# Window attention with routed experts: rows kept in 32-feature blocks, and slots turned in place by VectorE

## The chip, the cores and the metric

The kernel runs on one core of a Trainium2 chip. The metric is the device time of one execution in microseconds (us). Before the change three runs took 627.72, 629.17 and 631.42 us, a median of 629.17 us.

The engines are TensorE (PE in the profile; PEld is its weight loads), VectorE (DVE), ScalarE (ACT), GpSimd (POOL) and SyncE (SP), which issues most of the DMAs. SBUF is the memory on the core, with 128 partitions; PSUM is where PE writes its results.

## The reference

First a causal attention with a window of 64 over q, k, v of shape (8, 8, 576, 64); then each of the 4608 rows of 512 features goes through one of eight experts, chosen by a router.

```python
scores = scale * np.matmul(q, k.transpose(0, 1, 3, 2))
rel = pos[:, None] - pos[None, :]
mask = (rel >= 0) & (rel < window)
scores = np.where(mask, scores, -1000000000.0)
...
x = np.ascontiguousarray(attn_out.transpose(0, 2, 1, 3)).reshape(B * S, H * D)
logits = x @ w_gate + modality_bias[modality_id]
e_idx = np.argmax(logits, axis=1)
...
for e in range(E):
    mask = e_idx == e
    h = np.maximum(x[mask] @ w1[e], 0.0)
    out[mask] = gate_w[mask, None] * (h @ w2[e])
```

Here w1 is (8, 512, 1024) and w2 is (8, 1024, 512).

## The kernel before

**Attention steps.** Time goes in steps `s`. Step `s` forms the scores of 128 rows (`scores`, L647), their masked minima (`minima`, L661) and exponentials; one step later PE transposes the exponentials (`probs_t`, through `turn`, L481), two steps later come the values (`values`, L699) and `values_out`, which divides by the sums and writes the 128 rows as `xa` (L707, 128x512). PE transposes `xa` (`x_t`) and `logits` multiplies with the gate weights `wg` and adds the bias into `lg` (L729). Transposes, logits and routing share the PSUM banks `tp`, taken in turn, two of them; a bank that one reader still needs holds up the next writer. Tiles keep the same few names in the whole program (`tp`, `em`, `y`, `sp`), since buffers are used again.

**Routing.** `route1` to `route3` choose the expert and the place of each row. GpSimd writes the rows, `ROW` = 514 floats each (512 features, the gate value, the row's number), to `xs_scratch` in DRAM by an indirect DMA (L800). Each expert owns a region there.

**Slots.** A slot is 256 rows of one expert. `fetch` asks for the next slot and `load_slot` (L214, on SP) brings its rows into `xt`, of which there is one buffer. `slot_pieces` is a generator: from step `FIRST` = 12 on, four of its pieces are run in the gaps of each step (`gap`), between pieces of attention, and a slot takes 16 pieces. When the attention is over (about 340 us), slots run alone up to the end. There are 17 full slots and one of 128 rows.

The rows of a slot must have features on partitions for PE. A float32 product is made of three, with each operand split into a high part and a rest (`split`: ScalarE's cast L195, VectorE's subtraction L196; `xh` and `xl`). `first` multiplies with w1 (L318), ScalarE takes the positive part `hh` (L326), VectorE makes its rest `hl` (L327), and `second` multiplies with w2 (L340). The weights come in chunks of 128x512 floats (`load_piece`, L103), and are split too (L114, L119).

How `xt` is turned depends on when the slot is fetched. While `last` is not set, which holds for the first eight slots, `xt` comes in one DMA, and PE transposes it in two groups of four 128x128 pieces into PSUM (`x_turn`, L281), each with every fourth feature (`xt[:, t, c:DM:NC1]`); w1 is stored to match, in the order `(p c)`. Later slots come in four quarters of 32 partitions and one small DMA for the last two columns, and VectorE turns their 32x32 blocks into PSUM (L276). The casts of x are appended to `later`, a list which `run_later` empties at the end of a gap, behind what the gap's matmuls need.

The attention's q and k are loaded by SP too (L591 and, for the later groups, eight DMAs in quarters, L597); VectorE turns those quarters with one transpose of 128x512 (L575). Each engine works through its own instructions in the order of the program, and so does SP with its DMA issues.

```python
sl = fetch()
x_part(sl, 0)
x_part(sl, 1, ps_m.tile([P, 512], F32, name="y1"))
```

This is how the first slot starts, at step 12.

Of the kernel before, what the change touches and what calls it, by code (L numbers as in the profile page):

```python
# [8 lines left out]
F32 = mybir.dt.float32  # L9
F32R = mybir.dt.float32r  # L10
# [9 lines left out]
P = 128  # L20
# [6 lines left out]
def tile_window_attn_moe(  # L27
# [63 lines left out]
    Wlo = [wpool.tile([P, 2 * WC], F32R, name=f"Wlo{x}") for x in range(2)]  # L91


    w1_v = w1.rearrange("e (p c) f -> e p c f", p=P)
    w2_v = w2.rearrange("e (c p) f -> e p c f", p=P)

    PIECE_ORDER = (0, 2, 4, 6, 8, 9, 1, 3, 5, 7, 10, 11, 12, 13, 14, 15)
# [102 lines left out]
        assert (sl["buf"], c) not in pieces + [r[1:] for r in raws + halves]  # L200
        assert sl["any"] is None or (sl["any"], c) not in [w[2:] for w in swaps]

    def load_slot(row_ap, late, nb, quarters):
        rb = nc.values_load(row_ap, engines=[ET.SP], min_val=0, max_val=DUMMY)
        xt = epool.tile([P, 2, ROW], F32, name="xt")
        rows = xs_blk[bass.ds(rb, nb)]
        if not quarters:
            parts = [(xt[:, 0:nb], rows.rearrange("b p c -> p b c"))]
        else:
            parts = [(x_of(xt)[r * R32:(r + 1) * R32, 0:nb].rearrange("p b w d c -> p b w (d c)"),  # L210
                      rows[:, :, r * P:(r + 1) * P].rearrange("b (w p) c -> p b w c", p=R32)) for r in range(NR)]
            parts.append((tail_of(xt)[:, 0:nb], rows[:, :, DM:ROW].rearrange("b p c -> p b c")))
        for dst, src in parts:
            ins = nc.sync.dma_start(out=dst, in_=src)  # L214
            if late is not None:
                tc.declare_no_dep(ins.ins, group=late, reason="rows written before are read")
                tc.add_to_no_dep_group("early_loads", ins.ins)
        return xt

    def x_of(xt):  # L220

        flat = xt.rearrange("p b c -> p (b c)")
        return flat[:, 0:2 * DM].rearrange("p (b w d c) -> p b w d c", b=2, d=R32, c=NC1)
# [26 lines left out]
    def fetch():  # L250
        if fetched:
            return fetched.pop(0)
        row, late, buf, whichever, need = todo.pop(0)
        assert late is not None or not pads
        assert late is None or late in scattered
        tick(need - issued[0], table=True)
        nb = 1 if whichever == NANY else 2
        quarters = bool(last)
        xt = load_slot(row, late, nb, quarters)
        return dict(xt=xt, buf=buf, any=whichever, nb=nb, quarters=quarters,  # L260
                    tail=tail_of(xt) if quarters else xt[:, :, DM:])

    def slot_pieces():


        def x_turn(sl, i, tp=None):

            xt, nb = sl["xt"], sl["nb"]
            if ("tp", i) in sl or nb == 1 and i == 0:
                return  # L270
            tp = sl["tp", i] = tp or bank(2 if i and (last or not sl["quarters"]) else 0)
            cs_ = range(2 * i, 2 * i + 2) if nb == 2 else range(NC1)
            for n, c in enumerate(cs_):
                cols = slice(n * nb * P, (n + 1) * nb * P)
                if sl["quarters"]:
                    nc.vector.transpose(  # L276
                        out=tp[:, cols].rearrange("p (w t) -> p w t", t=R32),
                        in_=x_of(xt)[:, 0:nb, :, :, c].rearrange("p b w d -> p (b w) d"))
                    continue
                for t in range(nb):  # L280
                    nc.tensor.transpose(  # L281
                        out=tp[:, cols][:, t * P:(t + 1) * P].bitcast(F32R),
                        in_=xt[:, t, c:DM:NC1].bitcast(F32R), identity=ident_r)

        def x_split(sl, i):

            nb = sl["nb"]
            x_turn(sl, i)
# [4 lines left out]
            hi, lo = (x[:, (2 * i * TP if nb == 2 else 0):][:, 0:512] for x in sl["x"])  # L293
            split(sl.pop(("tp", i)), hi, lo)
            if i == 1:
                sl["gate"] = epool.tile([P, 2], F32, name="gate", bufs=2)
                nc.gpsimd.tensor_copy(out=sl["gate"][:, 0:nb], in_=sl["tail"][:, 0:nb, 0])
                sl["id"] = epool.tile([P, 2], I32, name="id", bufs=2)
                nc.gpsimd.tensor_copy(out=sl["id"][:, 0:nb], in_=sl["tail"][:, 0:nb, 1])

        def x_part(sl, i, tp=None):
            if not sl["quarters"]:
                x_turn(sl, i, tp)
            later.append(lambda: x_split(sl, i))
# [77 lines left out]
        def half_second(sl, a):  # L382
# [5 lines left out]
            for m, (w, n, c, lo) in enumerate(mm):  # L388
# [5 lines left out]
                    start=(m == 0), stop=(m == len(mm) - 1))  # L394
            id2 = epool.tile([P, 1], I32, name=f"id{a}")
            nc.gpsimd.tensor_scalar(
                out=id2, in0=sl["tail"][:, 0, 1:2], scalar1=2.0, scalar2=float(a),
                op0=ALU.mult, op1=ALU.add)

            def out_():  # L400
# [12 lines left out]

        sl = fetch()
        x_part(sl, 0)
        x_part(sl, 1, ps_m.tile([P, 512], F32, name="y1"))
        yield
        first(sl, 0, 0)
        yield
# [3 lines left out]
        while True:  # L423
            nxt = None
            for k in range(1, NK):
                for i in range(2):
                    if (k, i) == ((1, 0) if last else (2, 1)) or k == 2 and i == 1 and nxt is None:
                        assert todo
                        nxt = fetch()
                    first(sl, k, i)  # L430
                    if k == NK - 1 and i == 0 and last and nxt["quarters"]:
                        later.append(lambda: (x_turn(nxt, 0), x_turn(nxt, 1)))
                    yield
                for t in range(2):
# [268 lines left out]
    def values_out(p):  # L703
        rs = st.pop((p, "rs"))
        nc.vector.reciprocal(out=rs, in_=rs)
        xa = st[p, "xa"] = xas[p % XBUF]
        nc.vector.tensor_tensor(  # L707
            out=xa[:, 0:DM].rearrange("p (h d) -> p h d", d=D), in0=st.pop((p, "av")),
            in1=rs[:, :, None].broadcast_to([P, H, D]), op=ALU.mult)
# [323 lines left out]
    nc.scalar.dma_start(out=wg, in_=w_gate.rearrange("(c p) e -> p c e", p=P))  # L1033
# [13 lines left out]
    for s in range(NPR + 4):  # L1047
# [244 lines left out]
    with tc.If(trip > 0):  # L1292
        NS = N // P + E
        with ExitStack() as gctx:
# [38 lines left out]
            with tc.For_i(0, trip, 1) as it:  # L1333
# [77 lines left out]
```

## Time and profile before

| what | value |
|---|---|
| median of three runs | 629.17 us |
| profiled execution | 628.87 us |
| its span in the trace | 627.1 us |
| mean granted clock of PE | 0.995 of full speed |
| steps without slots | up to about 75 us |
| steps with slots | about 75 to 340 us |
| slots alone | about 340 us to the end |

The page shows the busy time of each engine in 40 equal slices (a digit is tenths, 9 means 90% or more):

```profile
PE   8899889899999999999999999999999999999996
DVE  4889878667667776766645266324334743876721
ACT  4899785565656555545462111111113522564411
DMA  9999846755567555575412132632322652587400
```

One slice is 15.7 us. PE is full nearly everywhere; VectorE, ScalarE and the DMA engines are full only in the first slices, before the slots begin. A row of a group or of the timeline names the line, engine, operation, `out<-in` and the shape; what stands in brackets is the engine's idle time before it, with the work that ended the idle time.

### The profile page before, as it was taken

The numbers are of one execution on the slowest core, as the hardware profiler recorded it, in microseconds if no ns is written. First come the engines' busy times: TensorE is split into PE (matmuls) and PEld (weight loads), VectorE is DVE, ScalarE is ACT, GpSimd is POOL, SyncE is SP. The second block draws the span as 40 slices with busy tenths as digits, with TensorE's granted clock in tenths as the row PEclk, the third lists the DMA queues.
The fourth block names the chain that finished last, engine by engine and source line by source line (L and its number), as shares of the span: only waits on it lengthen the run. The fifth ranks groups of instructions, "written<-read, shape, count | busy, mean of one in ns | idle before, by whom it ended". The sixth has DMA issues, their size and how long they took to land.

```text
span 627.1 us, 17384 instructions
## 1 busy us (share of the span) xinstructions
PE 604.4 (96%) x6349; PEld 541.4 (86%) x6349; DVE 390.1 (62%) x1503; ACT 292.0 (47%) x923; POOL 136.9 (22%) x315
## 2 busy tenths in 40 slices
PE   8899889899999999999999999999999999999996
PEld 5788778788879888989898899999999999989986
DVE  4889878667667776766645266324334743876721
ACT  4899785565656555545462111111113522564411
POOL 6422412132222222321323120011011011101102
PEclk9999999899999999999999999999999999999998
DMA  9999846755567555575412132632322652587400
GB/s 181 213 246 236 227 120 155 192 151 166 123 147 198 140 117 138 141 157 102 131 51 90 48 102 79 229 97 68 98 104 82 195 162 95 191 238 230 138 12 25
DMA packets 174039, 88.09 MB, mean 140 GB/s; under 512 B 143818, under 2 KB 154624, under 8 KB 173824
## 3 DMA queue, kind: packets, MB, share of 16 engines
q1 hardware_dynamic: 165376, 67.46, 44.0%
q0 software_dynamic: 5888, 18.93, 8.0%
q8 instruction: 50, 0.82, 0.6%
q10 hardware_dynamic: 2688, 0.58, 0.5%
q14 instruction: 37, 0.30, 0.2%
HBM read 67.49 MB, written 23.91 MB: 146 GB/s over the span
## 4 chain that ended last, share of the span: by engine, by line
PE 79%; ACT 0%; issue 0%; DVE 0%; POOL 0%; POOLq 0%; ACTq 0%
PE y L340 30%; PE em L318 20%; PE sp L318 10%; PE tp L481 7%; PE av L699 4%; PE sp L647 3%; PE tp L724 1%; PE y L391 1%; PE em L281 1%; PE tp L281 0%; PE sp L366 0%; PE em L366 0%; ACT ss L673 0%; ACT pT L682 0%; DVE hl L327 0%
## 5 line engine op out<-in xcount | busy, mean ns | idle before, releaser
L340 PE MATMUL y<-Whi,hh 128*128 128x512 f32 x288 | 116.1, 403 | 0.0
L673 ACT ACTIVATE ss<-ss,mn 128x128 f32<-128x128 f32 x288 | 112.5, 397 | 2.2 <-DVE mn L661 2.2
L340 PE MATMUL y<-Wlo,hh 128*128 128x512 f32 x288 | 113.1, 393 | 0.0
L340 PE MATMUL y<-Whi,hl 128*128 128x512 f32 x288 | 112.6, 391 | 0.0
L351 POOL DMA_INDIRECT out_dram<-y,id x36 | 37.4, 1038 | 249.0 <-DVE y L348 165.4
L327 DVE SCALAR_TENSOR_TENSOR hl<-em,hh 128x512 fp32r<-128x512 f32 x50 | 34.5, 689 | 85.3 <-ACT hh L326 81.8
L318 PE MATMUL em<-xh,Whi 128*128 128x256 f32 x400 | 83.7, 290 | 0.0
L318 PE MATMUL em<-xl,Whi 128*128 128x256 f32 x400 | 79.1, 279 | 0.0
L318 PE MATMUL em<-xh,Wlo 128*128 128x256 f32 x400 | 79.1, 279 | 0.0
L326 ACT ACTIVATE hh<-em 128x512 fp32r<-128x512 f32 x50 | 29.5, 591 | 106.1 <-PE em L318 102.1
L661 DVE CUSTOM_DVE_ANT_0 ss<-sp,masks 128x128 f32<-128x128 f32 x288 | 63.6, 286 | 9.1 <-PE sp L647 7.6
L682 ACT COPY pT<-tp 128x512 f32<-128x512 f32 x57 | 31.5, 590 | 74.3 <-PE tp L481 73.4
L340 PEld LDWEIGHTS y<-Whi,hl 128*128 128x128 f32 x288 | 54.3, 188 | 12.1
L318 PEld LDWEIGHTS em<-xh,Whi 128*128 128x128 f32 x400 | 62.3, 189 | 2.0 <-DVE xl L196 0.2
L340 PEld LDWEIGHTS y<-Whi,hh 128*128 128x128 f32 x288 | 54.4, 189 | 8.6
L340 PEld LDWEIGHTS y<-Wlo,hh 128*128 128x128 f32 x288 | 54.4, 189 | 8.3
L318 PEld LDWEIGHTS em<-xl,Whi 128*128 128x128 f32 x400 | 60.8, 188 | 0.0
L318 PEld LDWEIGHTS em<-xh,Wlo 128*128 128x128 f32 x400 | 60.8, 188 | 0.0
L673 ACT ACTIVATION_READ_ACCUMULATOR ss<-ss,mn 128x1 f32 x288 | 55.6, 193 | 0.0
L800 POOL DMA_INDIRECT xs_scratch<-xa,idx x36 | 36.3, 1009 | 79.8 <-DVE lm L743 24.1
L326 ACT ACTIVATE hh<-sp 128x512 fp32r<-128x512 f32 x22 | 13.1, 597 | 76.0 <-PE sp L318 74.0
L699 PEld LDWEIGHTS av<-ve,pT 128*64 128x64 f32 x576 | 36.3, 138 | 11.7 <-issue 6.7
(253 smaller groups left out, 1212.1 us busy)
## 6 DMA issues: line engine op xcount, KB each, us to landing
vo<-in_v_dram SPq DMA_DIRECT2D x32, 256.0 KB
y<-in_moe_w_dram SPq DMA_DIRECT2D x32, 256.0 KB
vo<-in_moe_w_dram SPq DMA_DIRECT2D x24, 256.0 KB
ss<-in_moe_w_dram SPq DMA_DIRECT2D x24, 256.0 KB
xt<-xs_scratch SPq DMA_DIRECT2D x40, 128.0 KB
xt<-xs_scratch SPq DMA_DIRECT2D x8, 514.0 KB
xs_scratch<-xs_scratch SPq DMA_DIRECT2D x8, 514.0 KB
pT<-in_moe_w_dram SPq DMA_DIRECT2D x16, 256.0 KB
```

Source lines behind the costliest of these rows:

```text
L318: nc.tensor.matmul(out=hb[:, i * TP:(i + 1) * TP], lhsT=w[buf][:, c0:c0 + P], rhs=x[:, c * TP:(c + 1) * TP], start=(n == 0), stop=(n == le ...
L326: nc.scalar.activation(out=hh, in_=hb, func=AF.Relu),
L327: nc.vector.scalar_tensor_tensor(out=hl, in0=hb, scalar=0.0, in1=hh.bitcast(F32), op0=ALU.max, op1=ALU.subtract)))
L340: nc.tensor.matmul(out=sl["y", t], lhsT=h[:, i * TP + t * P:i * TP + (t + 1) * P], rhs=w[buf][:, c0:c0 + DM], start=(k == 0 and n == 0), s ...
L351: ins = nc.gpsimd.indirect_dma_start(out=out, out_offset=bass.IndirectOffsetOnAxis(ap=sl["id"][:, t:t + 1], axis=0), in_=y, in_offset=None ...
L481: nc.tensor.transpose(out=out_, in_=in_, identity=ident[p0:p0 + n, p0:p0 + n])
L647: nc.tensor.matmul(out=sp[a][c * W64:(c + 1) * W64, hp * P:(hp + 1) * P], lhsT=qT[rows, place(g + c, hp), :], rhs=kT[rows, win(c, hp), :], ...
L661: nc.vector.tensor_tensor_reduce(out=ss[a][:, hp, :], in0=sp[a][:, hp * P:(hp + 1) * P], in1=mask, scale=-1.0 / 8.0, scalar=3.0e38, op0=AL ...
L673: nc.scalar.activation(out=ss[a][:, hp, :], in_=ss[a][:, hp, :], func=AF.Exp, bias=mn[:, h:h + 1], scale=-1.0, accum_out=sm[:, h:h + 1])
L682: nc.scalar.copy(out=pT, in_=pp)
L699: nc.tensor.matmul(out=av[c * W64:(c + 1) * W64, 2 * hp + a], lhsT=pT[:, i:i + W64], rhs=(vo if c else ve)[p][:, 2 * hp + a, :], start=Tru ...
L800: ins = nc.gpsimd.indirect_dma_start(out=xs, out_offset=bass.IndirectOffsetOnAxis(ap=idx[:, j:j + 1], axis=0), in_=xg[j], in_offset=None)
```

## The change

1. `values_out` writes the features of a row in another order: 32-feature blocks, so that the quarter `r` of a row (128 columns) holds the features `c*128 + r*32 + d` for all four `c`. Two instructions over half the elements each do it in place of one.
2. `load_slot` loads every slot by quarters: each of four DMAs brings one quarter of all rows, 512 B runs, to 32 partitions, and a fifth the last two columns.
3. `x_turn` is now two VectorE transposes of 128x512 in place, which turn each 32x32 block. For the slot at step 12 it stands ahead of `minima`; in the early slots it comes behind the last `hl` before the new slot; in the late ones where the turning stood before. PE's transposes of `xt` are gone.
4. The casts read the turned `xt` in SBUF; the PSUM banks that held it aren't taken. `xt` is free again only when they are done.
5. The features of chunk `c` are now 128 in a row, so w1's chunks are read as `(c p)`: each partition's run of 2 KB lies 4 KB from the next one's instead of 16 KB. The gate weights are put in the order of `xa` by four DMAs on ScalarE's queue instead of one.

The general loop for a table that doesn't fit (`gxt`) is changed to match; it doesn't run with these inputs.

```diff
-    w1_v = w1.rearrange("e (p c) f -> e p c f", p=P)
+    w1_v = w1.rearrange("e (c p) f -> e p c f", p=P)
...
-        if not quarters:
-            parts = [(xt[:, 0:nb], rows.rearrange("b p c -> p b c"))]
-        else:
-            parts = [(x_of(xt)[r * R32:(r + 1) * R32, 0:nb].rearrange("p b w d c -> p b w (d c)"),
-                      rows[:, :, r * P:(r + 1) * P].rearrange("b (w p) c -> p b w c", p=R32)) for r in range(NR)]
-            parts.append((tail_of(xt)[:, 0:nb], rows[:, :, DM:ROW].rearrange("b p c -> p b c")))
+        parts = [(x_of(xt)[r * R32:(r + 1) * R32, 0:nb].rearrange("p b w c d -> p b w (c d)"),
+                  rows[:, :, r * P:(r + 1) * P].rearrange("b (w p) c -> p b w c", p=R32)) for r in range(NR)]
+        parts.append((tail_of(xt)[:, 0:nb], rows[:, :, DM:ROW].rearrange("b p c -> p b c")))
...
+    def x_turn(sl):
+
+        nb = sl["nb"]
+        flat = sl["xt"].rearrange("p b c -> p (b c)")
+        for b in range(nb):
+            nc.vector.transpose(out=flat[:, b * DM:(b + 1) * DM], in_=flat[:, b * DM:(b + 1) * DM])
...
-        def x_turn(sl, i, tp=None):
...
-                for t in range(nb):
-                    nc.tensor.transpose(
-                        out=tp[:, cols][:, t * P:(t + 1) * P].bitcast(F32R),
-                        in_=xt[:, t, c:DM:NC1].bitcast(F32R), identity=ident_r)
...
+            raw = x_of(xt)[:, 0:nb].rearrange("p b w c t -> p c (b w) t")[:, cs_]
+            hi, lo = (x[:, cs_.start * nb * P:][:, 0:512].rearrange("p (c w t) -> p c w t", w=nb * NR, t=R32)
+                      for x in sl["x"])
+
+            def out_():
+                split(raw, hi, lo)
...
         sl = fetch()
         x_part(sl, 0)
-        x_part(sl, 1, ps_m.tile([P, 512], F32, name="y1"))
+        x_part(sl, 1)
...
-                    if k == NK - 1 and i == 0 and last and nxt["quarters"]:
-                        later.append(lambda: (x_turn(nxt, 0), x_turn(nxt, 1)))
+                    if k == NK - 1 and i == (0 if last else 1):
+                        later.append(lambda: x_turn(nxt))
...
-        nc.vector.tensor_tensor(
-            out=xa[:, 0:DM].rearrange("p (h d) -> p h d", d=D), in0=st.pop((p, "av")),
-            in1=rs[:, :, None].broadcast_to([P, H, D]), op=ALU.mult)
+        av = st.pop((p, "av")).rearrange("p (c g) (a d) -> p a c g d", g=2, a=2)
+        to = xa[:, 0:DM].rearrange("p (g a c d) -> p a c g d", g=2, a=2, d=R32)
+        for a in range(2):
+            nc.vector.tensor_tensor(
+                out=to[:, a], in0=av[:, a],
+                in1=rs.rearrange("p (c g) -> p c g", g=2)[:, :, :, None].broadcast_to([P, NC1, 2, R32]), op=ALU.mult)
...
-    nc.scalar.dma_start(out=wg, in_=w_gate.rearrange("(c p) e -> p c e", p=P))
+    for c in range(NC1):
+        nc.scalar.dma_start(
+            out=wg[c * R32:(c + 1) * R32],
+            in_=w_gate[c * P:(c + 1) * P].rearrange("(r d) e -> d r e", d=R32))
...
             if s == FIRST:
+                x_turn(fetched[0])
                 gap(it, True)
```

What moves is shown at three places. The rows give line, operation, `out<-in` and shape, and a count where one row stands for several instructions.

On PE, at the end of the slot that runs before 250 us (the products with w2 behind its last `hl`, up to the values of the next step), stood before:

```order
L340 MATMUL y_4486<-Whi_65,hl 128x512
L281 MATMUL em<-ident_r,xt 128x128 x4
L340 MATMUL y_4501<-Whi_65,hh 128x512
L340 MATMUL y_4501<-Wlo_66,hh 128x512
L340 MATMUL y_4501<-Whi_65,hl 128x512
L340 MATMUL y_4501<-Whi_65,hh 128x512
L340 MATMUL y_4501<-Wlo_66,hh 128x512
L340 MATMUL y_4501<-Whi_65,hl 128x512
L281 MATMUL tp<-ident_r,xt 128x128 x4
L699 MATMUL av<-ve,pT 64x64
```

And now:

```order
L326 MATMUL y_4497<-Whi_65,hl 128x512
L326 MATMUL y_4512<-Whi_65,hh 128x512
L326 MATMUL y_4512<-Wlo_66,hh 128x512
L326 MATMUL y_4512<-Whi_65,hl 128x512
L326 MATMUL y_4512<-Whi_65,hh 128x512
L326 MATMUL y_4512<-Wlo_66,hh 128x512
L326 MATMUL y_4512<-Whi_65,hl 128x512
L685 MATMUL av<-ve,pT 64x64
```

Both groups of four transposes are gone, and nothing takes their place on PE.

On VectorE, at the same place (the last `hl`, then the routing's `cnt` and `tgt`, the turn of q, and the routing's next steps), stood before:

```order
L327 SCALAR_TENSOR_TENSOR hl<-em,hh 128x512
L848 SCALAR_TENSOR_TENSOR e_used<-e_av,e_used 1x1
L825 COPY cnt<-tp 1x8
L781 TENSOR_TENSOR tgt<-tp,ebase 128x16
L575 STREAM_TRANSPOSE qT<-qk 128x512
L786 TENSOR_REDUCE se<-ex 128x2
L787 TENSOR_TENSOR tgt<-tgt,oh 128x16
L788 TENSOR_SCALAR se<-se 128x2
L790 TENSOR_REDUCE dst<-tgt 128x2
L794 RECIPROCAL xa_103<-se 128x1
L794 RECIPROCAL xa_104<-se 128x1
L196 TENSOR_TENSOR xl<-em,xh 128x512
```

And now:

```order
L313 SCALAR_TENSOR_TENSOR hl<-em,hh 128x512
L266 STREAM_TRANSPOSE xt<-xt 128x512 x2
L837 SCALAR_TENSOR_TENSOR e_used<-e_av,e_used 1x1
L814 COPY cnt<-tp 1x8
L770 TENSOR_TENSOR tgt<-tp,ebase 128x16
L561 STREAM_TRANSPOSE qT<-qk 128x512
L775 TENSOR_REDUCE se<-ex 128x2
L776 TENSOR_TENSOR tgt<-tgt,oh 128x16
L777 TENSOR_SCALAR se<-se 128x2
L779 TENSOR_REDUCE dst<-tgt 128x2
L783 RECIPROCAL xa_103<-se 128x1
L783 RECIPROCAL xa_104<-se 128x1
```

The two transposes of `xt` stand ahead of the routing and of the turn of q; the rests `xl` follow behind, as before.

On SP, at the fetch issued at 197 us (its row's number is loaded first; `vo` and `qk` are the attention's v, k and q), stood before:

```order
L204 TENSOR_LOAD rows_4125
L204 ISA x2
L214 ISA
L214 DMA xt<-xs_scratch 128x2x514
L540 DMA vo<-in_v_dram 128x8x64
L591 DMA qk<-in_k_dram 96x4x64 x2
```

And now:

```order
L211 ISA
L211 DMA xt<-xs_scratch 32x8x128
L211 ISA
L211 DMA xt<-xs_scratch 32x8x128
L211 ISA
L211 DMA xt<-xs_scratch 32x8x128
L211 ISA
L211 DMA xt<-xs_scratch 32x8x128
L211 ISA
L211 DMA xt<-xs_scratch 128x2x2
L526 DMA vo<-in_v_dram 128x8x64
L577 DMA qk<-in_k_dram 96x4x64 x2
```

Five issues, each with an instruction of its own ahead of it, stand where one stood, ahead of the next loads of v, k and q.

More of the change, by code (lines that the diff above doesn't have):

```diff
@@ L201, in ready, with load_slot @@
         assert sl["any"] is None or (sl["any"], c) not in [w[2:] for w in swaps]
-    def load_slot(row_ap, late, nb, quarters):
+    def load_slot(row_ap, late, nb):
         rb = nc.values_load(row_ap, engines=[ET.SP], min_val=0, max_val=DUMMY)
@@ L222, in x_of, with runs_of @@
         flat = xt.rearrange("p b c -> p (b c)")
[L223 removed]
+        return flat[:, 0:2 * DM].rearrange("p (b w c d) -> p b w c d", b=2, d=R32, c=NC1)
+    def runs_of(x):
+        return x[:, 0:DM].rearrange("p (r c d) -> p r c d", r=NR, d=R32)
     def tail_of(xt):
@@ L257, in fetch, with x_part @@
         nb = 1 if whichever == NANY else 2
[L258 to L261, printed above, removed]
+        return dict(xt=load_slot(row, late, nb), buf=buf, any=whichever, nb=nb)
+    def x_turn(sl):
[3 more added lines that the diff above has]
+            nc.vector.transpose(out=flat[:, b * DM:(b + 1) * DM], in_=flat[:, b * DM:(b + 1) * DM])
     def slot_pieces():
-        def x_turn(sl, i, tp=None):
+        def x_part(sl, i):
             xt, nb = sl["xt"], sl["nb"]
[L269 to L279, printed above, removed]
-                for t in range(nb):
-                    nc.tensor.transpose(
-                        out=tp[:, cols][:, t * P:(t + 1) * P].bitcast(F32R),
-                        in_=xt[:, t, c:DM:NC1].bitcast(F32R), identity=ident_r)
-        def x_split(sl, i):
-            nb = sl["nb"]
-            x_turn(sl, i)
             if i == 0:
@@ L292, in x_split @@
                     return
[L293 to L304, printed above, removed]
+            cs_ = slice(2 * i, 2 * i + 2) if nb == 2 else slice(0, NC1)
+            raw = x_of(xt)[:, 0:nb].rearrange("p b w c t -> p c (b w) t")[:, cs_]
[3 more added lines that the diff above has]
+                split(raw, hi, lo)
+                if i == 1:
+                    sl["gate"] = epool.tile([P, 2], F32, name="gate", bufs=2)
+                    nc.gpsimd.tensor_copy(out=sl["gate"][:, 0:nb], in_=tail_of(xt)[:, 0:nb, 0])
+                    sl["id"] = epool.tile([P, 2], I32, name="id", bufs=2)
+                    nc.gpsimd.tensor_copy(out=sl["id"][:, 0:nb], in_=tail_of(xt)[:, 0:nb, 1])
+            later.append(out_)
         def first(sl, k, i):
@@ L396, in half_second @@
             nc.gpsimd.tensor_scalar(
-                out=id2, in0=sl["tail"][:, 0, 1:2], scalar1=2.0, scalar2=float(a),
+                out=id2, in0=tail_of(sl["xt"])[:, 0, 1:2], scalar1=2.0, scalar2=float(a),
                 op0=ALU.mult, op1=ALU.add)
@@ L1339, in tile_window_attn_moe @@
                 xp = gps.tile([P, 512], F32, name="gxp")
+                xo = gen.tile([P, DM], F32, name="gxo")
+                nc.vector.tensor_copy(
+                    out=xo.rearrange("p (c r d) -> p r c d", r=NR, d=R32), in_=runs_of(xt))
                 for c in range(NC1):
-                    nc.tensor.transpose(out=xp[:, c * P:(c + 1) * P], in_=xt[:, c:DM:NC1], identity=ident)
+                    nc.tensor.transpose(out=xp[:, c * P:(c + 1) * P], in_=xo[:, c * P:(c + 1) * P], identity=ident)
                 xT = gen.tile([P, DM], F32, name="gxT")
```

## The prediction, made before the changed kernel ran

> **What bounds the kernel now.** I read the page's totals, then the chain that ended last, then the windows of the stages, then the waits and single instructions at the places that the change touches.
>
> ```profile
> span 627.1 us, 17384 instructions
> PE 604.4 (96%) x6349; PEld 541.4 (86%) x6349; DVE 390.1 (62%) x1503; ACT 292.0 (47%) x923; POOL 136.9 (22%) x315
> PE 79%; ACT 0%; issue 0%; DVE 0%; POOL 0%; POOLq 0%; ACTq 0%
> ```
>
> TensorE (PE) is busy for 96% of the span and carries 79% of the chain. The windows say where that is not the whole truth (columns: stretch, then its length, PE, PEld, DVE, ACT and POOL busy with counts, granted clock, DMA share, GB/s):
>
> ```profile
> 20.00:40.00 20.00, 19.17 (x400) 17.61 (x399) 17.62 (x99) 19.03 (x78) 5.71 (x13) 1.00 0.97 220
> 40.00:60.00 20.00, 17.87 (x334) 15.75 (x334) 18.39 (x105) 19.14 (x74) 8.22 (x16) 1.00 1.04 253
> 165.00:208.00 43.00, 41.43 (x534) 37.12 (x534) 30.98 (x141) 25.65 (x90) 10.70 (x22) 1.00 0.64 159
> 250.00:292.00 42.00, 41.96 (x560) 37.84 (x558) 28.28 (x141) 22.76 (x85) 10.70 (x22) 1.00 0.62 141
> 380.00:610.00 230.00, 230.00 (x1487) 209.28 (x1486) 121.81 (x209) 68.57 (x126) 26.26 (x61) 1.00 0.45 137
> ```
>
> Three stages have three limits. Before slots run (20 to 60 us) VectorE and ScalarE are nearly full and PE is not. From about 75 to 340 us, attention steps and slots together, PE is nearly full, with stalls at single places. From about 340 us PE alone is the limit: 230.00 of 230 us.
>
> **The change, part by part.** All terms are against the profiled execution, 628.87 us (span 627.1 and what lies around it); the median shown is 629.17 us, 0.30 more.
>
> *Values in blocks.* Each of the 36 steps writes `xa` by two half-size instructions instead of one:
>
> ```profile
> 51.41 0.20 DVE L705 RECIPROCAL rs<-rs 128x8 f32<-128x8 f32 x1
> 51.70 0.69 DVE L707 TENSOR_TENSOR xa<-av,rs 128x512 f32<-128x512 f32 x1
> 52.31 0.15 DVE L729 TENSOR_TENSOR lg<-y,bias_sel 128x8 f32<-128x8 f32 x1
> 7.67 0.42 DVE L628 COPY kT<-tp 128x256 f32<-128x256 f32 x1 [6.45 <-PE tp L481]
> 8.01 0.41 DVE L628 COPY qT<-tp 128x256 f32<-128x256 f32 x1
> ```
>
> A whole one holds VectorE for 0.61 us (51.70 to 52.31). Halves of that size start 0.34 apart, so an overlapping pair costs 0.34 x 2 = 0.68, 0.07 more. But the second half waits for the semaphore of the first; if it starts only after the first's end with a 0.09 us gap (51.61 to 51.70 is the like gap ahead of the row shown), the pair costs 0.42 + 0.09 + 0.34 = 0.85, 0.24 more. I take 0.24, since the order shows that wait. It is on the path only where VectorE is the limit: some 6 steps of about 10 us in 20 to 75 us, 6 x 0.24 = **+1.4 us** (bounds 0.07 x 6 = +0.4 and 0.24 x 10 = +2.4). Later it lies beside PE, except where PE waits for `lg`, below.
>
> *The gate weights* come in four issues on ScalarE instead of one, at the start.
>
> ```profile
> 9.17 0.41 ACTq L1033 DMA_DIRECT2D wg<-in_moe_w_gate_dram  x1
> 10.21 0.40 ACT L673 ACTIVATE ss<-ss,mn 128x128 f32<-128x128 f32 x1 [1.36 <-DVE mn L661]
> ```
>
> Three more at 0.41 are 1.23 us, and ScalarE has 10.21 - 9.58 = 0.63 of idle time behind the first. At most 0.6 shows, ahead of a stage with room on PE: I take 0, with +0.6 as the other end.
>
> *Rows loaded in quarters.* For the eight early slots, five SP issues replace one.
>
> ```profile
> 152.66 0.40 SPq L214 DMA_DIRECT2D xt<-xs_scratch  x1
> 197.34 0.40 SPq L214 DMA_DIRECT2D xt<-xs_scratch  x1
> 219.98 5.26 SPq L597 DMA_DIRECT2D qk<-in_q_dram  x8
> 396.30 2.51 SPq L214 DMA_DIRECT2D xt<-xs_scratch  x5
> 400.88 1.33 DVE L276 STREAM_TRANSPOSE em<-xt 128x256 f32<-128x256 f32 x2 [0.51 <-DMA xt<-xs_scratch]
> ```
>
> The late slots do this already: five issues take 2.51 us against 0.40, so each early fetch holds SP for **2.1 us** more. The data lands 2.07 us behind the last issue (398.81 to 400.88). SP's timeline is without a gap worth naming from 152.66 to about 276 us, since it issues the q and k loads there, so what is queued behind each fetch is late by 2.1, and behind two fetches by 4.2. Who waits:
>
> ```profile
> 227.22 0.69 DVE L575 STREAM_TRANSPOSE qT<-qk 128x512 f32<-128x512 f32 x1
> 229.71 1.10 PE L647 MATMUL sp<-kT,qT 64*64 64x128 f32 x32
> ```
>
> The last issue of that q ends at 225.24; with landing 2.07 it is there at 227.31, when VectorE takes it, so the transfer has no slack on VectorE beyond perhaps 1 us. It has 229.71 - 227.91 = 1.8 us up to PE's scores. Late by 4.2, the scores are late by 4.2 - 1.8 = 2.4, or 1.4 where that 1 us is there. I take **+2.0 us** (ends 0 and +2.4).
>
> The Trainium skill, "DMA: Bandwidth & Descriptors", section "Anatomy of one DMA", gives every DMA a fixed cost of about 2.0 us, mostly the wait for the completion. Paid one after the other that would be 8 us more per fetch, and the sum would be some 47 us higher (8 slots of 8 - 2.1); the trace has five issues 0.5 us apart and about 2 us once behind the last, so the row decides, and the page agrees with the landing only.
>
> *The second slot (115 us)* waits for SP in another way:
>
> ```profile
> 117.17 1.57 SPq L103 DMA_DIRECT2D y<-in_moe_w_dram  x3
> 119.84 0.62 ACT L114 CAST Whi<-y 128x512 fp32r<-128x512 f32 x1 [4.22 <-DMA y<-in_moe_w_dram]
> 120.97 0.69 DVE L196 TENSOR_TENSOR xl<-em,xh 128x512 fp32r<-128x512 f32 x1 [3.54 <-ACT xh L195]
> 122.32 2.14 PE L481 MATMUL tp<-ident_r,ss 128*128 128x128 f32 x8 [2.32 <-DVE xl L196]
> ```
>
> Weights land late, ScalarE waits 4.22 us for them, its cast of x stands behind, VectorE's `xl` behind that, and PE 2.32 us behind `xl`. SP being later by 2.1 moves this whole chain; turning x earlier gains nothing on it. The `xa` pair adds nothing that 2.1 does not cover; part may be taken up at the head of the chain. **+1.9 us** (ends 0 and +2.4).
>
> *Who turns x.* PE's eight transposes per early slot go, and VectorE does two in-place ones ahead of its other work. The slot at 247 us:
>
> ```profile
> 246.17 0.68 DVE L327 SCALAR_TENSOR_TENSOR hl<-em,hh 128x512 fp32r<-128x512 f32 x1
> 246.99 0.69 DVE L575 STREAM_TRANSPOSE qT<-qk 128x512 f32<-128x512 f32 x1
> 247.62 0.11 DVE L786 TENSOR_REDUCE se<-ex 128x2 f32<-128x16 f32 x1
> 246.95 0.73 PE L281 MATMUL em<-ident_r,xt 128*128 128x128 f32 x4
> 247.52 0.46 PE L340 MATMUL y<-Whi,hh 128*128 128x512 f32 x1
> 248.99 0.63 PE L281 MATMUL tp<-ident_r,xt 128*128 128x128 f32 x4
> 249.54 0.27 PE L699 MATMUL av<-ve,pT 128*64 128x64 f32 x1
> 250.27 0.69 DVE L196 TENSOR_TENSOR xl<-tp,xh 128x512 fp32r<-128x512 f32 x1 [1.24 <-ACT xh L195]
> 251.77 0.15 DVE L729 TENSOR_TENSOR lg<-tp,bias_sel 128x8 f32<-128x8 f32 x1
> 252.08 1.09 PE L481 MATMUL tp<-ident_r,ss 128*128 128x128 f32 x8
> 87.82 0.66 PE L481 MATMUL tp<-ident_r,ss 128*128 128x128 f32 x4 [1.16 <-DVE lg L729]
> ```
>
> PE is rid of what stands between the start of each group and that of its next matmul: 247.52 - 246.95 and 249.54 - 248.99, 0.57 + 0.55 = 1.12 us. A transpose of 128x512 on VectorE takes 0.69 by the `qT` row, 0.63 up to the next instruction, so the pair adds 1.26. That is just what VectorE idles in front of its second `xl` (1.24), because x is now whole earlier: `xl` still ends near 250.96, and `lg`, with the `xa` pair, at 252.16 instead of 251.92. PE comes 1.12 earlier to the eight transposes of `ss`, but the second four of them need the bank that `lg` reads; the row at 87.82 us shows PE waiting just there. In the run of before they begin near 252.5, half way through the eight; now at about 252.25, when `lg` and its semaphore are through. Of 1.12 us, **0.25** is left; 0.9 is a new wait of PE for `lg`.
>
> The slots at 161 and 204 us have the same form and gain 0.1 to 0.25 each, which the late q takes (it sets the scores behind them). The first slot (75.8 us) trades PE transposes for VectorE ones ahead of the minima that PE also waits for: 0. At 286 us 0.25 again. At 330 and 361 us less stands behind `lg`:
>
> ```profile
> 360.14 0.77 PE L281 MATMUL em<-ident_r,xt 128*128 128x128 f32 x4
> 362.21 0.63 PE L281 MATMUL tp<-ident_r,xt 128*128 128x128 f32 x4
> ```
>
> At 361 no attention runs, PE keeps 1.1 us. At 330 I estimate 0.7, between 0.25 and 1.1. Together 0.25 + 0.25 + 0.7 + 1.1 = **-2.3 us** (ends 0 and -9.0, which is eight times 1.12).
>
> By the Trainium skill, "VectorE: DVE Perf Modes", section "Rules for kernel authors", a 128x128 transpose is TensorE's wherever PSUM will do, and 32x32 blocks are VectorE's. By the rows either engine takes 0.6 to 0.7 us for 128x512, so the rule would leave the -2.3 out (+5.3 in all); the placing decides, not the rate.
>
> *Late slots.* Four VectorE transposes of half size become two:
>
> ```profile
> L276 DVE STREAM_TRANSPOSE tp<-xt 128x256 f32<-128x256 f32 (+1 forms) x24 | 14.2, 592 | 0.4
> ```
>
> That is 4 x 0.59 against 2 x 0.69, about 1 us per slot of VectorE, which has 108 us free in the 230: 0. The weight chunks change addresses alone, with the same bytes and issues: 0, though a late chunk would show at PE.
>
> **Sum:** 628.87 + 1.4 + 0 + 2.0 + 1.9 - 2.3 = **631.9 us**, +0.5% on the profiled execution and +0.4% on the median. A measurement of this kernel tells about 0.5% from no change (under 626.0 or over 632.3).
>
> **Rivals.**
>
> 1. *PE's load governs.* The new wait for `lg` does not arise, since VectorE's chain moves up with x, and SP's lateness is hidden: then PE's transposes come off in all slots but the first, 628.9 + 1.4 - 7 x 1.12 = **622.5 us**. For it: 41.96 of 42 us. Against: the 1.16 us wait at 87.82.
> 2. *The queue does not matter.* q and the weights still land in time, because SP makes up the 2.1 us in its own waits. Then 628.9 + 1.4 - 2.3 - 0.4 for the two middle slots = **627.6 us**. For it: SP leads its users by some us elsewhere; against: 227.22 and the wait of 4.22.
> 3. *Rows land late* (the other side, clearly slower). VectorE is in order: if x is not there when the turn comes, `tgt`, the turn of q, `xl`, `xa` and `lg` all stand behind it, and PE behind them. With SP late by 4.2, a fetch at 239.03 starts at 243.2, ends its issues at 245.7 and lands at 247.8, against a turn at 246.8. It decides as soon as SP is later than 3.2 us while the rest of the kernel is not; a price of 2 us in each of five slots (161 to 330) on top of +1.4 - 2.3 gives 628.9 + 10 - 0.9 + 1.9 = **640 us**.
>
> **How the numbers follow.** Forecast 0.45, rival 2 0.30, rival 1 0.13, rival 3 0.12. Of the forecast's own spread half lies within 0.5% and half above; rival 2 lies within it, save 0.05 below. So faster 0.13 + 0.05 = 0.18, same 0.25 + 0.22 = 0.47, slower 0.23 + 0.12 = 0.35. The range reaches from 622.0, just past rival 1, to 636.5, where the terms' upper ends lie without PE's gain (628.9 + 2.4 + 0.6 + 2.4 + 2.4 = 636.7); rival 3 and the tails of the others are left outside, not quite 0.2.
>
> **What would show it.** In the changed profile, L281's rows are gone; the turn's pair should take 1.26 us, an `xa` half 0.42, the five issues 2.5 us. Right for the forecast: PE waits of some 0.9 us for `lg` behind the slots at 161, 204, 247 and 286, a longer wait at 115 to 122, and scores near 230 late by about 2. Wrong: steps with slots shorter by over 1 us (rival 1), no lateness near 230 (rival 2), VectorE waiting for `xt` at the turn (rival 3), or a stall of PE for weights after 380.

## The result, and the profile after

The changed kernel takes 634.34 us (median of 8 runs, 631.66 to 636.49), the kernel before in the same set 629.05 us (8 runs, 627.52 to 631.94). The ratio of the means is 1.0074, with a 95% interval of 1.0044 to 1.0103: slower by 0.7%; the medians lie 5.3 us apart. The profiled execution took 633.95 us.

The page's totals and four stretches of the windows view (columns as in the prediction: stretch, length, busy time and count of PE, PEld, DVE, ACT and POOL, granted clock, DMA share, GB/s) of the changed kernel:

```profile
span 632.2 us, 17434 instructions
PE 601.1 (95%) x6285; PEld 536.4 (85%) x6285; DVE 390.4 (62%) x1532; ACT 294.3 (47%) x923; POOL 139.5 (22%) x315
0.00:20.00 20.00, 16.89 (x180) 12.22 (x180) 10.22 (x63) 9.71 (x36) 10.00 (x54) 0.83 0.88 164
122.00:165.00 43.00, 37.74 (x445) 33.93 (x444) 29.31 (x133) 24.34 (x84) 9.78 (x20) 0.92 0.63 157
208.00:250.00 42.00, 38.15 (x500) 33.08 (x499) 30.34 (x142) 20.93 (x75) 11.29 (x22) 0.96 0.57 135
380.00:610.00 230.00, 230.00 (x1497) 209.66 (x1496) 110.08 (x199) 69.50 (x127) 28.49 (x60) 1.00 0.46 137
```

PE has 64 instructions less and is 3.3 us less busy, yet the span is 5.1 us longer: most of the loss is idle time of PE, and a lower clock, in the second and third of these stretches. In the same two the kernel before shows:

```profile
122.00:165.00 43.00, 42.26 (x509) 37.73 (x511) 31.72 (x141) 25.64 (x90) 11.18 (x22) 0.96 0.57 142
208.00:250.00 42.00, 41.32 (x537) 37.15 (x534) 30.33 (x145) 23.41 (x86) 11.04 (x22) 1.00 0.58 142
```

PE is busy for 4.5 us less in the one and 3.2 in the other; the stretches don't hold quite the same work, since steps have moved. Where the time went is read best from the starts of the scores (L647 before, L633 after), which mark each step. The table sums the lengths of the steps, in us; the differences add up to the 5.1 us of the spans.

| stretch | before | after | difference | forecast |
|---|---|---|---|---|
| up to the scores of step 3 | 23.89 | 25.66 | +1.8 | 0 |
| steps 3 to 11 (no slots) | 50.84 | 50.96 | +0.1 | +1.4 |
| steps 12 to 18 (first and second slot) | 78.71 | 81.81 | +3.1 | +1.9 |
| steps 19 to 25 (161 and 204 us, late q) | 76.27 | 78.85 | +2.6 | +2.0 |
| steps 26 to 34 | 93.04 | 92.90 | -0.1 | -0.5 |
| step 35 to the end | 304.38 | 302.04 | -2.3 | -1.8 |

The steps within show both sides of it. The five steps that end with turning a slot (15, 19, 23, 27, 31) are shorter by 1.40, 1.59, 1.58, 1.16 and 1.16 us, 6.9 together. The steps behind them give 1.41 (20), 0.88 (24), 0.50 (28) and 0.43 (32) back. Step 16 takes 18.35 instead of 14.05 us, and step 25 15.17 instead of 11.06.

Step 16, the second slot, in the timeline of the changed kernel (SP's queue, then ACT, DVE and PE; what stands in brackets is the wait ahead):

```profile
109.53 3.87 SPq L211 DMA_DIRECT2D xt<-xs_scratch  x5
121.21 2.46 SPq L103 DMA_DIRECT2D y<-in_moe_w_dram  x3
124.92 0.62 ACT L114 CAST Whi<-y 128x512 fp32r<-128x512 f32 x1 [5.66 <-DMA y<-in_moe_w_dram]
126.49 0.58 ACT L668 COPY pT<-tp 128x512 f32<-128x512 f32 x1
126.09 1.29 DVE L196 TENSOR_TENSOR xl<-xt,xh 128x512 fp32r<-128x512 f32 x2 [4.17 <-ACT xh L195]
128.39 0.15 DVE L718 TENSOR_TENSOR lg<-tp,bias_sel 128x8 f32<-128x8 f32 x1
127.12 1.11 PE L467 MATMUL tp<-ident_r,ss 128*128 128x128 f32 x4 [4.99 <-ACT pT L668]
128.46 0.63 PE L326 MATMUL y<-Wlo,hh 128*128 128x512 f32 x1
```

It is the chain of before, longer and with another end: five issues took 3.87 us, the weights behind them landed late, ScalarE waited 5.66 us for them instead of 4.22, and PE 4.99 instead of 2.32. Before, PE's wait ended with `xl`; here it ended with the copy `pT`, which stands behind the casts on ScalarE. PE's transposes started at 127.12, ahead of `lg` at 128.39, so they did not take the bank that `lg` reads. Then PE is slow: a product takes 0.63 us where it takes 0.40 at the full clock, and the granted clock was 0.50 from 124.9 to 131.6 us (its row is in the last section).

Step 25, the late q:

```profile
229.21 5.24 SPq L583 DMA_DIRECT2D qk<-in_q_dram  x8
230.39 0.30 PE L467 MATMUL tp<-ident_r,qk 128*128 128x128 f32 x1 [2.01 <-DMA qk<-in_q_dram]
236.05 0.71 DVE L561 STREAM_TRANSPOSE qT<-qk 128x512 f32<-128x512 f32 x1 [2.67 <-DMA qk<-in_q_dram]
232.37 0.63 PE L326 MATMUL y<-Wlo,hh 128*128 128x512 f32 x1
```

SP's last issue of this q ends at 234.45, 9.2 us later than before, where steps have moved by 3.5 (222.11 against 218.66 at the start of step 25). VectorE waits 2.67 us for it, and PE had waited 2.01 us for the other half of q already, with slow products behind (granted clock 0.50 from 230.7 to 234.0 us).

Behind the turned slots PE waits for `lg`, here at 171 and 260 us:

```profile
171.46 0.63 PE L467 MATMUL tp<-ident_r,ss 128*128 128x128 f32 x4 [1.20 <-DVE lg L718]
259.84 0.63 PE L467 MATMUL tp<-ident_r,ss 128*128 128x128 f32 x4 [0.31 <-DVE lg L718]
```

### The profile page after: what moved, and what is told of

Same layout as the page of the kernel before. It is cut to its first block, busy times and chain, and to the rows that moved or that the text cites. A ratio compares the mean times of both kernels' runs of the same rounds, so it can differ in the third digit from the quotient of the medians.

```text
span 632.2 us, 17434 instructions
## 1 busy us (share of the span) xinstructions
PE 601.1 (95%) x6285; PEld 536.4 (85%) x6285; DVE 390.4 (62%) x1532; ACT 294.3 (47%) x923; POOL 139.5 (22%) x315
## 4 chain that ended last, share of the span: by engine, by line
PE 50%; DVE 0%; issue 0%; POOL 0%; ACT 0%; POOLq 0%
PE y L326 23%; PE em L304 13%; PE sp L304 10%; PE tp L467 1%; PE y L377 1%; PE av L685 1%; PE sp L352 0%; PE em L352 0%; PE tp L713 0%; PE sp L633 0%; DVE xa L696 0%; POOL out_dram L390 0%; ACT pT L668 0%; POOLq L1284 0%; DVE y L388 0%
## 5 line engine op out<-in xcount | busy, mean ns | idle before, releaser
L337 POOL DMA_INDIRECT out_dram<-y,id x36 | 39.8, 1104 | 235.2 <-DVE y L334 154.9
L647 DVE CUSTOM_DVE_ANT_0 ss<-sp,masks 128x128 f32<-128x128 f32 x288 | 63.4, 285 | 5.0 <-PE sp L633 4.9
L467 PE MATMUL tp<-ident_r,ss 128*128 128x128 f32 x236 | 36.1, 284 | 12.3 <-ACT pT L668 8.4
```

Source lines behind the costliest of these rows:

```text
L337: ins = nc.gpsimd.indirect_dma_start(out=out, out_offset=bass.IndirectOffsetOnAxis(ap=sl["id"][:, t:t + 1], axis=0), in_=y, in_offset=None ...
L467: nc.tensor.transpose(out=out_, in_=in_, identity=ident[p0:p0 + n, p0:p0 + n])
L647: nc.vector.tensor_tensor_reduce(out=ss[a][:, hp, :], in0=sp[a][:, hp * P:(hp + 1) * P], in1=mask, scale=-1.0 / 8.0, scalar=3.0e38, op0=AL ...
```

## The experiments

Two theories were set against each other. **Theory A**: SP's queue, held longer by five issues in place of one, delays weights and q. **Theory B**: the short runs, or VectorE's turn, are what costs. The start and the wait for `lg` have tests of their own. Each ratio is to the kernel before on the same chip in the same set, whose medians were 628.75, 630.7, 628.84 and 629.73 us in the four sets.

### The one DMA of the kernel before cut into five

Into five groups of partitions, with the runs of 2056 B kept:

```diff
-            parts = [(xt[:, 0:nb], rows.rearrange("b p c -> p b c"))]
+            at5 = (0, 26, 52, 78, 104, P)
+            parts = [(xt[x:y, 0:nb], rows[:, x:y].rearrange("b p c -> p b c")) for x, y in zip(at5, at5[1:])]
```

> The kernel before, with the one DMA of each early slot cut into five by partitions: the same bytes, the same runs of 2056 B, five issues on SP instead of one. Theory A (SP's queue: an early fetch holds SP some 2.1 us longer, and the weights behind the second slot and the q of group 13 come too late): the step from 119 to 133 us (14.05 us in the kernel before) and the step from 219 to 230 us (11.06) grow by 2 to 4 us each, and the time by +4 to +8 us. Theory B (the loads are slow because of the short runs of 512 B, or the stalls come from VectorE's turn): no step grows by over 0.5 us and the time stays within 0.5%.

Measured: 634.76 us, ratio 1.0098 (1.0059 to 1.0137). Step 25 takes 16.15 us (+5.1), steps 15 and 16 together 27.58 instead of 25.92. Of these two it is step 15 that grew (14.94 instead of 11.87), since ScalarE waits for late weights there already, for 1.66 us; step 16 itself fell from 14.05 to 12.64, which was not expected. In its trace (SP, PE and DVE in step 25):

```profile
199.55 3.68 SPq L215 DMA_DIRECT2D xt<-xs_scratch  x5
228.91 0.86 PE L482 MATMUL tp<-ident_r,qk 128*128 128x128 f32 x3 [0.45 <-DMA qk<-in_q_dram]
232.37 0.71 DVE L576 STREAM_TRANSPOSE qT<-qk 128x512 f32<-128x512 f32 x1 [1.06 <-DMA qk<-in_q_dram]
```

And by columns, in runs of 512 B:

```diff
+            at5 = (0, P, 2 * P, 3 * P, DM, ROW)
+            parts = [(xt[:, 0:nb, x:y], rows[:, :, x:y].rearrange("b p c -> p b c")) for x, y in zip(at5, at5[1:])]
```

> The kernel before, with the one DMA of each early slot cut into four of 128 columns (runs of 512 B) and one of the last two: five issues and short runs, PE still turns x. Theory A: the same two steps grow by 2 to 4 us, as with the cut by partitions, to within 1 us. Theory B in its form of short runs: this one is slower than the cut by partitions by 2 us or more. Theory B in its form of VectorE's turn: neither grows.

Measured: 637.99 us, ratio 1.0152 (1.0112 to 1.0192). Steps 15 and 16 take 28.97 us, steps 25 and 26 24.71 instead of 21.06.

Five issues in place of one make the kernel before as slow as the changed one, with PE still turning x: theory A holds, and VectorE's turn isn't needed for the loss. But the cut by columns is 3.2 us slower than the cut by partitions, where theory A allowed 1: the short runs, or the fact that each of these five loads spreads over all partitions, cost something of their own there. Whether they do in the changed kernel, whose runs are also 512 B, stays open.

### SP relieved

v is loaded by ScalarE from step 12 on:

```diff
-            nc.sync.dma_start(out=t, in_=v_v[g0 // BPB, s0:s0 + P])
+            (nc.scalar if p >= FIRST else nc.sync).dma_start(out=t, in_=v_v[g0 // BPB, s0:s0 + P])
```

> The changed kernel, with the loads of v issued by ScalarE instead of SP from step 12 on; SP gets 0.4 to 0.6 us per step back, 1.6 to 2.4 per slot. Theory A: steps 16 and 25 (18.35 and 15.17 us in the changed kernel) fall by 2 to 4 us each, the other steps stay to within 0.5, and the time falls by 4 to 7 us. Theory B: both steps stay, and the time stays or grows, since ScalarE has 0.4 us more per step.

Measured: 631.96 us, ratio 1.0049 (1.0024 to 1.0073). Step 25 is 11.06 us again, all of the 4.1 gone; step 16 fell only to 17.14, step 26 rose by 1.5 to 11.93, and steps 28 and 32 by 0.4 and 0.5. This bears out theory A for step 25; for step 16 SP's gain is too small. The median is 2.4 us below the changed kernel's, less than was expected, and the intervals of the two ratios overlap.

The same in the kernel before:

> The kernel before, with v issued by ScalarE from step 12: a control. If giving SP time back helps only where an early fetch has five issues, the time stays within 0.4% of the kernel before, and steps 16 and 25 (14.05 and 11.06 us) change by less than 0.7. If SP's queue limited the kernel before as well, step 16 falls by 1 us or more and the time by 1 to 3 us.

Measured: 627.6 us, ratio 0.9937 (0.9914 to 0.9961). Step 16 takes 11.39 us instead of 14.05, step 25 10.98 instead of 11.06. SP's queue cost the kernel before some time too, so what this edit gains does not speak for the changed layout.

### What PE waits for behind a turned slot

The two subtractions for `xl` are held back until `logits` of the next step has run:

```diff
-                split(raw, hi, lo)
+                nc.scalar.copy(out=hi, in_=raw)
+                rest = lambda: nc.vector.tensor_tensor(out=lo, in0=raw, in1=hi.bitcast(F32), op=ALU.subtract)
+                if FIRST < now[0] < NPR - 1:
+                    rests.append(rest)
+                else:
+                    rest()
...
+        while rests:
+            rests.pop(0)()
         if s < NPR:
             scores(s)
```

> The changed kernel, with the two subtractions for xl of each slot that begins in the attention moved behind the values, the logits and lg of the next step (VectorE's order alone). Theory: PE's new wait behind a turned slot is for lg, which stands behind the turn, xl and xa on VectorE; then steps 20, 24, 28 and 32 (11.43, 10.91, 10.53, 10.46 us in the changed kernel) fall to 10.0 to 10.4 each, and the time by 1.5 to 3 us. Rival: those steps are longer because PE's work merely moved from the step before into them, or because of ScalarE's copies; then they stay to within 0.3 us, and the time too. Steps 16 and 25 wait for SP in either case and stay long.

Measured: 631.25 us, ratio 1.0021 (1.0001 to 1.0042). Steps 20, 28 and 32 fell from 11.43, 10.53 and 10.46 to 10.61, 10.02 and 10.08: the wait was for `lg`. But steps 21 and 29 behind them grew by 0.40 and 0.60, so that little of this gain is left. The gain of the whole comes from step 16, which did what was not expected: 13.71 instead of 18.35, though ScalarE still waits 4.66 us for its weights. In its trace `lg` now runs ahead of the `xl` that waits:

```profile
120.66 0.15 DVE L725 TENSOR_TENSOR lg<-tp,bias_sel 128x8 f32<-128x8 f32 x1
122.83 1.29 DVE L287 TENSOR_TENSOR xl<-xt,xh 128x512 fp32r<-128x512 f32 x2 [2.02 <-ACT xh L286]
120.96 0.63 PE L474 MATMUL tp<-ident_r,ss 128*128 128x128 f32 x4 [1.08 <-DVE lg L725]
```

PE's transposes now wait 1.08 us for `lg`, where they waited 4.99 us for `pT` in the changed kernel. So SP's lateness reached PE in step 16 through two engines that work in order: `pT` stood behind the casts on ScalarE, and `lg` behind `xl` on VectorE, and each of the two has a bank to read before PE may write it again. With `lg` ahead of `xl` one bank is free early, and the wait for `pT` that is left is 0.88 us. And step 24 shows the prediction's third rival, which the changed kernel itself does not:

```profile
204.85 1.31 DVE L268 STREAM_TRANSPOSE xt<-xt 128x512 f32<-128x512 f32 x2 [2.87 <-DMA xt<-xs_scratch]
```

With the earlier waits gone the step comes sooner, the rows aren't there when the turn comes, and step 24 takes 15.61 us. Step 25 takes 11.47 instead of 15.17: the two together, 27.08 us, are 1.0 longer than in the changed kernel.

Both edits together:

> Both edits of the changed kernel together: v issued by ScalarE from step 12, and xl behind lg. If SP's queue and the wait for lg are the two separate losses, the gains add: about 5 us below the changed kernel, 627 to 630 us, near the kernel before or 0.3% below it. If one only moves the other's wait, it stays at 630 to 633 us.

Measured: 626.61 us, ratio 0.9928 (0.9907 to 0.9949). Steps 16, 24 and 25 take 12.15, 10.68 and 11.80 us. The gains at least add, and this version is faster than the kernel before.

With the two plain loads of q and k per later group on ScalarE as well (`dma if G < QUARTERS else nc.scalar`):

> The changed kernel with v on ScalarE and xl behind lg, and besides the two plain DMAs of each later load of q and k (groups 8 and on) on ScalarE too, another 0.9 us per load off SP. If SP's queue still limits steps 24 to 26 (10.68, 11.80 and 11.50 us in the kernel with v on ScalarE and xl behind lg, where 10.0 to 10.4 is undisturbed), these three fall by 1 to 3 us together and the time by 1 to 3 us. If it is ScalarE's copies or VectorE's chain by now, they stay, and the time stays or grows by up to 2 us, since ScalarE issues 0.9 us more per load.

Measured: 633.58 us, ratio 1.0060 (1.0033 to 1.0088). The expected gain did not come: steps 24 to 26 take 37.08 us instead of 33.98. The timeline shows why:

```profile
211.09 4.35 ACTq L584 DMA_DIRECT2D qk<-in_q_dram  x4
215.49 1.07 ACT L675 COPY pT<-tp 128x512 f32<-128x512 f32 x2 [6.49 <-DMA qk<-in_q_dram]
216.12 1.11 PE L474 MATMUL tp<-ident_r,xa 128*128 128x128 f32 x4 [3.14 <-ACT pT L675]
```

The copies that PE needs stand behind four issues on ScalarE. The wait has changed its queue.

### The start

The four DMAs of the gate weights on GpSimd's queue (`nc.gpsimd.dma_start` in place of `nc.scalar.dma_start`):

> The changed kernel, with the four DMAs of the gate weights on GpSimd's queue instead of ScalarE's. Theory A for the start (2.42 us of issues on ScalarE ahead of the first exponentials): these begin near 10.3 us instead of 11.85, step 2 begins near 18 us instead of 19.5, and the time falls by 1 to 1.7 us. Rival: the start is late because PE's clock is low there after q and k landed 0.3 us later, by chance; then step 2 still begins later than 19 us, or varies with the clock of the first 20 us.

Measured: 635.82 us, ratio 1.0105 (1.0064 to 1.0146), not faster than the changed kernel. The exponentials begin at 10.85, but step 2 begins at 19.22, as the rival had it.

A longer warm-up, `WARM = 8, 6` in place of `8, 3`, on top of the two edits above:

> The changed kernel with v on ScalarE and xl behind lg, and six matmuls instead of three in the warm-up behind the first transposes of q and k. Theory for the start: wherever PE idles over 0.5 us before the second transposes of q and k (0.56 to 1.31 us in seven profiles so far), its clock is low up to 14 us and step 2 begins at 19.0 to 20.2 us, in kernels of both kinds; with PE kept busy there step 2 begins at 17.7 to 18.2 in the profile, and the time is 0.5 to 1.5 us below the same kernel without it. Rival: the changed kernel's start is late by the gate weights' issues on ScalarE; then step 2 still begins behind 19 us.

Measured: 629.52 us, ratio 1.0009 (0.9982 to 1.0037). PE is at full clock (the first scores take 1.10 us), and step 2 still begins at 19.69. In its trace:

```profile
9.96 3.56 ACTq L1030 DMA_DIRECT2D wg<-in_moe_w_gate_dram  x4
14.99 1.10 PE L640 MATMUL sp<-kT,qT 64*64 64x128 f32 x32 [1.97 <-ACT qT L621]
```

Here it is the gate weights: 3.56 us of issues, and PE waits 1.97 us for the copy behind them. Two causes can thus delay the start. One is PE's clock: the kernel before with v on ScalarE, whose gate weights are one DMA, shows it plainly,

```profile
7.09 0.71 PE L481 MATMUL tp<-ident_r,qk 64*128 64x64 f32 x8 [0.82 <-DMA qk<-in_k_dram]
8.53 1.99 PE L647 MATMUL sp<-kT,qT 64*64 64x128 f32 x32 [0.73 <-ACT kT L628]
```

with scores of 1.99 us instead of 1.10, a granted clock of 0.50 from 8.3 to 15.0 us, and step 2 at 19.16. The other is the four issues, worth 0.1 us in one profile at the full clock (the kernel with the plain loads on ScalarE, step 2 at 17.83 against 17.72 before) and up to 2.0 in the other.

### Single terms

The division of the values in two, in the kernel before:

```diff
+        for a in range(2):
+            hs = slice(a * HP, (a + 1) * HP)
+            nc.vector.tensor_tensor(
+                out=xa[:, a * DM // 2:(a + 1) * DM // 2].rearrange("p (h d) -> p h d", d=D), in0=av[:, hs],
+                in1=rs[:, hs, None].broadcast_to([P, HP, D]), op=ALU.mult)
```

> The kernel before, with the division of the values in two instructions over four heads each instead of one over eight. By the prediction's term (0.24 us per step where VectorE is the limit), steps 3 to 11 together (50.84 us in the kernel before) take 1.0 to 1.6 us longer. By the changed kernel's own steps 3 to 11 (50.96 us) the term is too large: 0 to 0.6 us longer, since most of these steps have some idle time on VectorE.

Measured: one run of 633.43 us; steps 3 to 11 take 50.76 us, 0.1 less than before, so the term is 0. The run's other 4.5 us of span are the start (1.7, at the low clock) and steps 23 to 29, two of which (26 and 29) are 0.9 and 1.3 us longer; a single run doesn't tell whether the second half of `xa` does that.

w1 in the old order, so that the products are others:

> The changed kernel with w1 read in the old order (every fourth row, runs of 2 KB at 16 KB instead of 4 KB); the features of x and w1 then don't match, so the products are others. If the order of the chunks costs or saves nothing, the stretch from step 35 to the end stays at 302.0 us to within 0.5, and no step from 12 on changes by over 0.5 us beyond steps 16 and 25 and their neighbours, which vary with the queue. If nearer runs help the loads, it grows by 1 us or more.

Measured: one run of 634.59 us; step 35 to the end takes 301.91 us against 302.04. The order of the chunks is worth nothing there. Step 33 took 13.70 us instead of 10.57; why stays open.

The version with both edits once more:

> The changed kernel with v on ScalarE and xl behind lg once more, since the one with the longer warm-up came out level with the kernel before (1.0009) and this one 0.7% below it (0.9928). If the longer warm-up cost the difference, the ratio is 0.990 to 0.995 again. If what differs is the set of runs, it comes out at 0.997 to 1.003.

Measured: 627.1 us, ratio 0.9957 (0.9935 to 0.9980), between the two ranges and again faster than the kernel before. The two sets put it 0.4 and 0.7% below the kernel before; against the kernel before with v on ScalarE (0.9937) no difference can be told.

## Why the forecast came out as it did

The time fell into the range and moved the way of the forecast, 2.4 us further than the sum (631.9). The terms were off in both directions, and that the sum came so near is in part luck: the +1.4 us for the values, worth 0.1, stood in for +1.8 us of start that was put at 0.

- **SP's queue, the term that decided**, was right in its mechanism: five issues delay what stands behind them, and the two places named are the two that grew. The stretch of steps 19 to 25 is +2.6 against +2.0. What the prediction did not see is how that sum is made: the two slots gained 3.2 us on PE, 2.3 came back in steps 20 and 24, step 21 is 0.6 shorter, and step 25 lost 4.1 with a wait of PE for the other half of q and a slower clock behind it. Counted from the start of step 25, SP's last issue of that q ended 5.8 us later than before (12.34 against 6.58), not 4.2. The section "Anatomy of one DMA" of the Trainium skill's page "DMA: Bandwidth & Descriptors", on which the prediction draws here, gives its 2.0 us for the path of DMAs that GpSimd issues, not for every DMA; these five are issued by SP, and for them only the rows count (2.07 us from the end of the last issue to the landing).
- **The second slot** was sized at +1.9 and measured +3.1. "Each early fetch holds SP for 2.1 us more" did not hold here, since the five issues took 3.87 us (0.40 before), 3.5 more. Yet the weights' first issue came just 2.1 us later, counted from the start of step 15 (12.24 against 10.15), because the ten issues of k between took 5.70 us instead of 7.66: that this part came out is luck. What the term missed lies behind it. The three issues of weights took 2.46 us instead of 1.57, the cast that waits for them stands 3.1 us later by the same count (15.95 against 12.82), and PE's six products behind the wait took 2.71 us instead of 2.17, as the low clock lasted longer (6.7 us against 3.3).
- **Who turns x** was right in its kind: PE's gain appears in full (1.16 us in step 27) and a wait for `lg` takes part of it back. By the prediction 0.25 of 1.12 us is left; measured are 0.2 at 161 us, and 0.7 at 204, 247 and 286 us. The pair of turns took 1.29 us as worked out, but VectorE's chain behind it was shorter: at 247 us `lg` ended 5.56 us behind the start of the last `hl`, where the working has 5.99 and the kernel before 5.75. So PE's waits for `lg` are 1.20, 0.31 and 0.24 us in steps 20, 28 and 32 and not 0.9 each; in step 24 PE waited 0.68 us for ScalarE's `pT` instead. The experiment with `xl` behind `lg` shows that the wait is that one.
- **The values in two** were sized at +1.4 and are worth 0 to 0.1. The pair does hold VectorE longer; the view of groups has it as

```profile
L696 DVE TENSOR_TENSOR xa<-av,rs 128x256 f32<-128x256 f32 x72 | 30.6, 425 | 10.1 <-PE av L685 4.9 <-DMA xs_scratch<-xa,idx 1.0 <-PE sp L633 0.4
```

  72 halves of 0.425 us, where one whole took 0.692. The step that failed is "it is on the path only where VectorE is the limit: some 6 steps": steps 8 to 11 are 0.10 to 0.19 us longer each, 0.5 together, and step 7 is 0.46 shorter. In the kernel before each of steps 3 to 11 has 0.14 to 0.98 us of idle time on VectorE, so none of them is its alone; that this idle time took up the rest is argued, not measured.
- **The gate weights** were put at 0 with an end of +0.6. That end was too low: four issues took 2.2 to 3.6 us instead of 4 x 0.41. How much of the start's +1.8 in the two profiles is theirs, and how much the clock's, stays open. The clock alone can make it: the granted clock from 9.0 to 15.5 us was 0.50 in the changed kernel's profile and 1.00 in that of before, and two profiles of the kernel before with one edit, with one DMA of gate weights and a clock of 0.50, began step 2 at 19.16 and 20.20 (17.72 before, 19.48 changed).
- **The late slots** gained 2.3 us from step 35 on, where -1.8 was forecast, and VectorE's lighter load (110.08 busy instead of 121.81 in the same stretch) cost and gained nothing, as said.
- **Rivals.** Rival 1 (PE's load governs) is refuted by the waits for `lg` and `q`. Rival 2 (the queue does not matter) is refuted by the cuts into five. Rival 3 (rows land late) is not in the changed kernel, where VectorE waits nowhere for `xt` at the early turns; it appeared, at 2.87 us, once another wait had been taken away.

## What to carry to other kernels

Count the issues of a change on the queue that works without a gap, and follow who stands behind them: here 2 to 3.5 us more per fetch on SP went with steps 16 and 25 being 8.4 us longer, more than the 6.0 us that sixteen groups of transposes, taken off the busiest engine, gave in the end. In-order engines pass a late transfer on to work that does not need it, so put what the bounding engine waits for (`lg`) ahead of what may be late (`xl`). And before moving issues to another engine, see whether that engine's next instruction is what the bounding engine waits for: v on ScalarE gained, the plain loads of q and k on top of it lost.

## What the runs showed of the hardware

The time that five issues take on SP isn't fixed: 2.45 to 2.52 us at most early fetches of the changed kernel, 3.87 at one, 5.21 in a variant (197.59 us in the kernel with the plain loads on ScalarE) and 6.22 in another (280.52 us in the second profile with both edits). One issue on ScalarE took 0.41 us in the kernel before, and 0.54 to 0.89 each for the four loads that follow each other at the start.

A wait of PE can cost more than its length, since the granted clock can fall with it. The windows view (columns as above) has, for the changed kernel and then the kernel before:

```profile
9.00:15.50 6.50, 6.50 (x72) 5.72 (x76) 4.62 (x27) 3.69 (x17) 2.17 (x8) 0.50 1.04 186
124.90:131.60 6.70, 4.48 (x15) 3.80 (x16) 5.21 (x26) 3.55 (x9) 0.00 (x0) 0.50 0.68 153
230.70:234.00 3.30, 3.02 (x12) 2.59 (x13) 1.50 (x5) 0.50 (x4) 0.00 (x0) 0.50 0.20 31
9.00:15.50 6.50, 6.19 (x101) 5.18 (x92) 5.62 (x39) 5.29 (x21) 2.03 (x8) 1.00 1.30 217
122.30:125.60 3.30, 3.28 (x12) 2.68 (x13) 2.94 (x20) 1.69 (x5) 0.00 (x0) 0.50 0.58 113
```

At 0.50 a product of 128x512 took 0.63 us instead of 0.40. Between 20 and 600 us of the fourteen profiles, each of the twelve waits of PE of 2.01 to 5.25 us has a stretch of 0.50 that begins within it or up to 0.5 us behind its end; of the fifteen waits of 1.66 to 2.00 us eight have one (up to 1.5 us behind), and of the shorter ones none. The wait of 1.97 us at the start of the kernel with the longer warm-up, shown above, has none either. In the start a wait of 0.56 to 1.31 us ahead of the second transposes of q and k was followed by first scores of 1.54 to 1.99 us instead of 1.10, in every profile that had one, of either kernel. The four profiles of experiments in which that row shows no wait had 1.10, and so had the kernel before with a wait of 0.37.
